# Attention feeding two MoE layers on one Trainium2 core: reciprocals one head later, transfers re-ordered, a third buffer pair, constants on GpSimd, an early weight split

## The chip, the cores and the metric

The kernel runs as one program on one core of a Trainium2 chip. The metric is the device time of one execution in microseconds: the median of three runs of the kernel before is 2205.02 us (2204.62 to 2205.92). Engines are named as in the profile: PE is TensorE, PEld its weight loads, DVE is VectorE, ACT is ScalarE, POOL is GpSimd, SP issues the transfers.

## The reference

Three parts, one behind the other, in float32 (moe_w_in and moe_w_out arrive as float64):

```python
# attention: B=4, H=8, S=576, D=64; a query sees the keys of its own and of earlier blocks of 64
scores = where(block_i >= block_j, q @ k.T / sqrt(D), -1e9)
attn = exp(scores - max(scores));  attn = attn / (sum(attn) + 1e-9);  out = attn @ v
# first MoE: x (2304, 512), w_in (512, 2048), w_out (2048, 512)
h = x @ w_in;  x = (h * cos(h)) @ w_out
# second MoE: 8 experts of width 1024, gates P from a softmax and 8 rounds of row and column normalisation
out = sum_e P[:, e] * (max(x @ w1[e], 0) @ w2[e])
```

## The kernel before, in words

**Order.** The program is written in the order in which each engine executes it; every engine works off its own instructions in that order and waits by semaphores for what an instruction reads, or for the last reader of what it overwrites. All transfers of the attention are issued from SP, also in that order, so a transfer that has to wait holds up those behind it.

**Precision.** Products are made from a rounded high part and a low part (the rest), in three passes (`mm3`, lines 469 to 472), so a matrix needs a high part (ACT as a rule) and a subtraction for the low part (POOL or DVE; `split`, line 61).

**Attention** (lines 147 to 463) takes the 32 heads one by one, in pairs: the even head h=0 and the odd head h=1 of a pair fill the upper and lower 64 rows of x. For head i:

- `load` brings q and k of a head, three heads ahead, into one of two buffers `st`; `load_v` brings v one head ahead.
- `high_parts` (ACT, and POOL for k into KA), `low_parts` (DVE) and `move_k_hi`, `move_k_lo`, `move_q_hi` (transfers between partitions) prepare the operands QA, KA, QB, KB of head i+2; there are two of each, slot i % 2. KA and QA also hold constants (mask, selectors) that `constants` writes once for each slot.
- `peak` is a cheap product into PSUM tile px, `find` on DVE reduces it to maxima, `turn` transposes them on PE, and `maxima` on DVE puts them as extra rows into QA, so that the score product itself subtracts them. That is done for head i+1 while head i runs. px is one buffer: the second group of `peak` waits for the first group's `find`.
- `weights` makes the scores in four parts, each with a first product (KB, QB; line 294) and a second (KA, QA; line 295, which needs the maxima) and an exponential on ACT. `pv` multiplies by v; one more column of ones gives the sums of the exponentials.
- `evac` copies the result to a RAW buffer (two pairs of buffers, by the pair's number), `sums` writes the row of sums to DRAM. Once a pair is complete, `fetch` reads both rows of sums back spread over 72 partitions (tile SC), `invert` takes the reciprocal on DVE, `give` writes them to DRAM, `spread` reads them back to all rows (tile RB, two transfers), `scale` multiplies RAW by RB into XF (DVE, one instruction for each half), and `x_hi` (ACT) and `x_lo` (POOL) split XF into the x of the MoE part.

The main loop is lines 408 to 455. In it, fetch and invert of a pair e stand in head e+2, invert behind the operands of the next head and right ahead of `maxima`; give and spread stand in head e+3, the two scales in heads e+4 and e+5, x_hi and x_lo in head e+5.

**Conversion.** The first MoE's weights arrive as 64-bit floats. `Conv` turns them into float32 in 32 half chunks, each by a load, two ACT, three DVE and one POOL instruction; its generator gives four steps for a half chunk, and `some(n)` takes n steps. Two steps fall into each head and five into each of the first units of the MoE part. Two scratch buffers alternate.

**Opening** (lines 385 to 407): loads, constants of slot 0 on DVE, the first head's operands and maxima, constants of slot 1 and further constants on DVE, then `turn(0)` and `maxima(0)`.

**First MoE** (lines 646 to 780): 48 units, each a block of 768 tokens by 128 columns of w_in: `hidden` twice (12 matmuls each into a buffer h, of which there are two), `reduce_h`, `sine` and `times` for h cos(h), then `o_part` adds the unit before to the output. `wsplit` splits weight chunks; the first stands at line 716, after the attention, followed by `gate_prep`, whose DVE instructions need the gate's transfer (line 487). What remains of the last pairs is done by the `leftover` steps at the ends of units 0 to 5 (lines 461 to 463).

**Second MoE**: from about 680 us on, not touched by the change.

Of the kernel before, what the change touches and what calls it, by code (L numbers as in the profile page):

```python
# [42 lines left out]
def attention_moe_kernel(ctx: ExitStack, tc: tile.TileContext, qk, v, w_a, gate, w_b, out):  # L43
# [10 lines left out]
    eps = top.tile([128, 2], F32, name="eps")  # L54
    nc.vector.memset(eps, 0.0)


# [9 lines left out]

    raw = [None] * F1


    NHALF = 2 * F1

    class Conv:
# [20 lines left out]
        def magnitude(self, k):  # L94

            self.sc[k] = self.scratch(1, k, [128, DM])
            nc.scalar.activation(self.sc[k].bitcast(F32), self.high(k).bitcast(F32), AF.Abs)
# [29 lines left out]
        def run(self):  # L127

            for k in range(NHALF):
                self.magnitude(k)  # L130
                self.rounding(k)
                if 0 < k < NHALF - 1:
                    self.load(k + 1)
                yield
                self.clamp(k)
                yield
                self.shift(k)
                yield
                self.bits(k)
                self.add(k)  # L140
                yield
# [5 lines left out]
    def attention():  # L147
        with tc.tile_pool(name="at1", bufs=1) as p1, tc.tile_pool(name="at2", bufs=2) as p2, \
# [21 lines left out]
            tla = post.tile([128, 6 * TB], F32, tag="tl", name="tla", bufs=1)  # L170
            RAW = [[tla[:, 2 * DM:2 * DM + S], p1.tile([128, S], F32, name="raw")],
                   [tla[:, 2 * DM + S:2 * DM + 2 * S], tt[0][:, 0:S]]]
            RB, XF = tt[1][:, 0:S], tt[2][:, 0:S]
            conv = Conv(post.tile([128, 4 * DM], I32, tag="th", name="cw", bufs=1), tla[:, 0:2 * DM].bitcast(I32))
            conv_gen = conv.run()
# [23 lines left out]

            def constants(slots):  # L200
                nc.vector.memset(diag, 0.0)
                step = [ident[64:72, a:a + 4].unsqueeze(2).to_broadcast([8, 4, 64]) for a in (64, 68)]
                blocks = lambda t, h: t[64:72, 64:576].rearrange("p (t h n) -> p t h n", h=2, n=64)[:, :, h, :]
                shifted = diag[64:72, 64:576].rearrange("p (t h n) -> p t h n", h=2, n=64)
                nc.vector.tensor_copy(out=shifted[:, :, 0, :], in_=step[1])
                nc.vector.tensor_copy(out=shifted[:, :, 1, :], in_=step[0])
                for j in slots:
                    nc.vector.tensor_copy(out=QA[j][:, 0:64], in_=diag[:, 0:64])
                    nc.vector.tensor_copy(out=QA[j][64:96, 64:640], in_=diag[64:96, 64:640])
                    nc.vector.tensor_scalar(out=KA[j][64:128, :], in0=diag[64:128, 0:S], scalar1=0.0, scalar2=None,  # L210
                                            op0=ALU.mult)
                    for h in range(2):
                        nc.vector.tensor_scalar(out=blocks(KA[j], h), in0=step[1 - h], scalar1=MASK, scalar2=None,
                                                op0=ALU.mult)
                    nc.vector.tensor_scalar(out=KA[j][96:101, :], in0=diag[96:101, 0:S], scalar1=-1.0, scalar2=None,
                                            op0=ALU.add)
                    nc.vector.memset(NM[j], 0.0)

            def more_constants():
                nc.vector.tensor_copy(out=diag[96:101, :].rearrange("p (t n) -> p t n", n=128),  # L220
                                      in_=ident[96:101, 96:101].unsqueeze(2).to_broadcast([5, 5, 128]))
                nc.vector.memset(V[0][:, :, D:D + 1], 1.0)
                nc.vector.memset(V[1][:, :, 0:D], 0.0)
                nc.vector.memset(V[1][:, :, 0:1], 1.0)

# [117 lines left out]
            def evac(i):  # L343
                m = D + 1 if i % 2 == 0 else 2 * D
                t = RAW[i // 2 % 2][i % 2]
                nc.scalar.activation(t[0:m], ps_o.pop(i)[0:m, 448:1024], AF.Identity, bias=eps[0:m, i % 2:i % 2 + 1])

            def sums(i):
                t, s = RAW[i // 2 % 2][i % 2], SUM[i % 2]
# [23 lines left out]
            def scale(e, h):  # L373
                r = slice(64 * h, 64 * h + 64)
                nc.vector.tensor_tensor(out=XF[r, :], in0=RAW[e // 2 % 2][h][r, :], in1=RB[r, :], op=ALU.mult)

# [13 lines left out]
            load_v(1)  # L390
            nc.scalar.activation(eps[:, 0:1], eps[:, 0:1], AF.Exp)
            constants([0])
            first_head()
            find(*peak(0, 0))
            find(*peak(0, 1))
            constants([1])
            high_parts(1)
            low_parts(1)
            more_constants()
            nc.vector.memset(eps, 0.0)  # L400
            nc.vector.memset(eps[D:D + 1, 0:1], EPS)
            nc.vector.memset(eps[0:1, 1:2], EPS)
            turn(0)
            maxima(0)
            move_k_hi(1)
            move_k_lo(1)
            load(2)
            for i in range(NH):
                nxt, even, odd = i + 1 < NH, i % 2 == 0, i % 2 == 1
# [46 lines left out]
            evac(NH - 1)  # L456
            e = NH - 2
            sums(NH - 1)
            scale(e - 2, 0)
            scale(e - 2, 1)  # L460
            return conv_gen, {0: lambda: (x_hi(e - 2), fetch(e)), 1: lambda: (invert(e), give(e), x_lo(e - 2)),
                              2: lambda: spread(e), 4: lambda: (scale(e, 0), scale(e, 1), x_hi(e)),
                              5: lambda: x_lo(e)}

    with tc.manual_schedule():
# [180 lines left out]
        def moe1():  # L646
            nonlocal th, tl, C0
            with tc.tile_pool(name="m1", bufs=2) as p, tc.tile_pool(name="pacc", bufs=1, space=PSUM) as pacc:
# [66 lines left out]

                wsplit(0, 0, nc.vector)
                gate_prep()
# [18 lines left out]
                for n in range(NU + 1):  # L736
# [253 lines left out]
```

## Time and profile before

| | |
|---|---|
| median of three runs | 2205.02 us |
| profiled execution | 2205.72 us |
| its span, first to last instruction | 2203.9 us |
| mean granted clock of TensorE | 0.993 |
| PE / PEld / DVE / ACT / POOL busy | 98 / 86 / 68 / 43 / 39 % |
| attention (first to last score product) | 16.6 to 250.5 us |
| first product of the MoE part | 258.4 us |

Busy shares are of the whole span. In the rows, a number in square brackets is the time for which the engine was idle just before, with what ended it. A granted clock of 1.00 is TensorE at 2.4 GHz, 0.50 would be a stretch wholly at 1.2 GHz, and values between are mixtures.

### The profile page before, as it was taken

How to read it: one execution, taken by the hardware profiler on the slowest of the kernel's cores; microseconds unless marked ns; L12 is line 12 of the kernel's file. 1: busy time of each engine (PE TensorE's matmuls, PEld its weight loads, DVE VectorE, ACT ScalarE, POOL GpSimd, SP SyncE). 2: the span in 40 equal slices, each digit the busy share in tenths (PEclk: the TensorE clock that was granted, in tenths of full speed). 3: DMA queues.
4: the chain of work that ended last, by engine and by line, in shares of the span. 5: the costliest groups of instructions: out<-in, count | busy, mean ns of one | idle time of the engine just before them, and what ended most of it. 6: DMA issues, size and time to landing. Idle time of an engine off the chain costs nothing.

```text
span 2203.9 us, 29623 instructions
## 1 busy us (share of the span) xinstructions
PE 2150.4 (98%) x10869; PEld 1889.4 (86%) x10869; DVE 1497.8 (68%) x2464; ACT 957.5 (43%) x1792; POOL 867.5 (39%) x766
## 2 busy tenths in 40 slices
PE   7888899999999999999999999999999999999999
PEld 5666689999898888888888888888888888888887
DVE  6777688666566876666767666666777666666665
ACT  5666555434444343433434434343434343433342
POOL 1222355333332343434563434343554343434341
PEclk9999999999999999999999999999999999999999
DMA  5676421000001121212122212121212221212120
GB/s 144 173 181 175 112 73 58 1 1 10 29 20 39 58 77 58 77 58 77 58 77 87 77 58 77 58 77 58 77 58 88 76 77 58 77 58 77 58 77 29
DMA packets 76641, 157.42 MB, mean 71 GB/s; under 512 B 33392, under 2 KB 33392, under 8 KB 76496
## 3 DMA queue, kind: packets, MB, share of 16 engines
q1 hardware_dynamic: 76496, 155.52, 23.1%
q8 instruction: 86, 1.41, 0.3%
q14 instruction: 59, 0.48, 0.1%
HBM read 136.91 MB, written 4.87 MB: 64 GB/s over the span
## 4 chain that ended last, share of the span: by engine, by line
PE 77%; DVE 7%; issue 7%; DMA 3%; ACT 3%; POOL 3%; SPq 1%; ACTq 0%; POOLq 0%; DVEq 0%
PE acc L470 12%; PE acc L472 12%; PE acc L471 12%; PE hx L472 6%; PE hx L470 6%; PE hx L471 6%; PE hy L472 3%; PE hy L470 3%; PE hy L471 3%; PE acc L701 3%; POOL jl L66 3%; DMA kb<-qb 1%; PE hz L470 1%; PE hz L472 1%; PE hz L471 1%
## 5 line engine op out<-in xcount | busy, mean ns | idle before, releaser
L580 POOL TENSOR_TENSOR wv<-stg,wv 128x512 fp32r<-128x512 f32 x190 | 333.7, 1778 | 858.5 <-ACT wv L579 858.5
L470 PE MATMUL acc<-wv,hh 128*128 128x512 f32 x1152 | 456.5, 396 | 0.0
L472 PE MATMUL acc<-wv,hl 128*128 128x512 f32 x1152 | 455.5, 395 | 0.0
L471 PE MATMUL acc<-wv,hh 128*128 128x512 f32 x1152 | 454.5, 395 | 0.0
L874 DVE SCALAR_TENSOR_TENSOR oa<-acc,P,oa 128x512 f32<-128x512 f32 x540 | 379.0, 740 | 4.9 <-PE acc L472 4.3
L845 ACT ACTIVATE hh<-c 128x384 fp32r<-128x384 f32 x288 | 151.4, 526 | 408.7 <-DVE c L930 167.8
L846 DVE SCALAR_TENSOR_TENSOR hl<-c,hh 128x384 fp32r<-128x384 f32 x288 | 164.0, 570 | 176.5 <-ACT hh L845 176.5
L472 PEld LDWEIGHTS acc<-wv,hl 128*128 128x128 f32 x1152 | 216.0, 187 | 53.7
L471 PEld LDWEIGHTS acc<-wv,hh 128*128 128x128 f32 x1152 | 215.9, 187 | 43.8
L470 PEld LDWEIGHTS acc<-wv,hh 128*128 128x128 f32 x1152 | 216.1, 188 | 43.0
L66 POOL TENSOR_TENSOR jl<-raw,jh 128x512 fp32r<-128x512 f32 x95 | 135.4, 1443 | 240.5 <-ACT jh L63 225.9
L923 DVE TENSOR_TENSOR c<-hz,c 128x384 f32<-128x384 f32 x96 | 53.5, 557 | 193.2 <-PE hz L472 193.2
L571 DVE TENSOR_TENSOR wal<-s,wah 128x1024 fp32r<-128x1024 f32 x96 | 171.4, 1785 | 0.0
L913 ACT ACTIVATE c<-hx 128x384 f32<-128x384 f32 x95 | 46.9, 493 | 275.5 <-PE hx L472 275.5
L470 PE MATMUL h<-xh,jh 128*128 128x384 f32 x384 | 130.5, 340 | 5.7 <-ACT jh L63 3.0
L472 PE MATMUL h<-xh,jl 128*128 128x384 f32 x384 | 129.9, 338 | 1.9 <-POOL jl L66 1.9
L673 ACT ACTIVATE r<-r,half_pi 128x384 f32<-128x384 f32 x96 | 59.2, 617 | 165.5 <-DVE r L668 164.7
L472 PE MATMUL hy<-xh,wal 128*128 128x384 f32 x384 | 128.8, 335 | 0.9 <-DVE wal L571 0.9
L471 PE MATMUL h<-xl,jh 128*128 128x384 f32 x384 | 129.2, 337 | 0.0
L470 PE MATMUL hx<-th,wah 128*128 128x384 f32 x384 | 128.6, 335 | 0.5 <-ACT c L913 0.5
L470 PE MATMUL hy<-xh,wah 128*128 128x384 f32 x384 | 128.7, 335 | 0.4 <-DVE c L930 0.2
L472 PE MATMUL hx<-th,wal 128*128 128x384 f32 x384 | 128.5, 335 | 0.0
(213 smaller groups left out, 4822.1 us busy)
## 6 DMA issues: line engine op xcount, KB each, us to landing
stg<-in_w_b_dram SPq DMA_DIRECT2D x192, 512.0 KB
cw<-in_w_a_dram SPq DMA_DIRECT2D x32, 512.0 KB
st<-in_qk_dram SPq DMA_DIRECT2D x64, 144.0 KB
v<-in_v_dram SPq DMA_DIRECT2D x31, 160.0 KB
tt<-inv SPq DMA_DIRECT2D x32, 144.0 KB
out_dram<-oa SPq DMA_DIRECT2D x18, 256.0 KB
kb<-hi SPq DMA_DIRECT2D x31, 144.0 KB
kb<-qb SPq DMA_DIRECT2D x31, 144.0 KB
```

The source lines that it names most:

```text
L66: eng_lo.tensor_tensor(out=lo, in0=src, in1=hi.bitcast(F32), op=ALU.subtract)
L470: nc.tensor.matmul(ps, lh, rh, start=first, stop=False, skip_group_check=go_on)
L471: nc.tensor.matmul(ps, lh, rl, start=False, stop=False, skip_group_check=go_on)
L472: nc.tensor.matmul(ps, ll, rh, start=False, stop=last, skip_group_check=go_on)
L571: eng.tensor_tensor(out=self.al, in0=self.s, in1=self.ah.bitcast(F32), op=ALU.subtract)
L580: eng.tensor_tensor(out=t[:, DM:2 * DM], in0=src, in1=t[:, 0:DM].bitcast(F32), op=ALU.subtract)
L673: nc.scalar.activation(r, r, AF.Sin, bias=half_pi)
L701: nc.tensor.matmul(acc[half, b][:, at:at + w_], w[:, s], h[:, t0:t0 + w_], start=f == 0 and i == 0 and at == 0, stop=f == F1 - 1 and i == ...
L845: nc.scalar.activation(hh, src, AF.Relu)
L846: nc.vector.scalar_tensor_tensor(out=hl, in0=src, scalar=0.0, in1=hh.bitcast(F32), op0=ALU.max, op1=ALU.subtract)
L874: nc.vector.scalar_tensor_tensor(out=o, in0=acc, scalar=p, in1=o, op0=ALU.mult, op1=ALU.add)
L923: nc.vector.tensor_tensor(out=c[0], in0=z, in1=c[0], op=ALU.add)
```

## The change

- `invert` moves from the even head e+2 (ahead of `maxima`) to the odd head e+3, behind the first `find` on DVE, with `give` right after it. `fetch` stays in head e+2, now ahead of `move_k_lo`; `spread` goes to the end of head e+3's transfers.
- `scale` of the first half moves to the end of head e+4, of the second half to the first part of head e+5; `x_hi` and `x_lo` to head e+6. RAW has three pairs of buffers, and room for them comes from one conversion scratch buffer instead of two and from a slot of the `post` pool.
- `load_v` and `load` stand at the head's start, ahead of `sums` and `move_q_hi`.
- The conversion's steps are cut differently (rounding with the clamp, bits with the shift, add alone), and the loop takes them at other places: one step fewer in head 0.
- In the opening the constants of slot 1, and the ones of v, are written by POOL; the selector tile is made once, the low part of head 1 comes after `maxima(0)`.
- The first weight chunk is split during head 31 into a part of x (xh and xl) that is written only later; the second chunk's split stands ahead of unit 0's products. The leftover steps of the last three pairs are spread over units 1 to 9.

```diff
@@ Conv.run
                 self.magnitude(k)
-                self.rounding(k)
                 if 0 < k < NHALF - 1:
                     self.load(k + 1)
                 yield
+                self.rounding(k)
                 self.clamp(k)
                 yield
                 self.shift(k)
+                self.bits(k)
                 yield
-                self.bits(k)
                 self.add(k)
                 yield
...
@@ opening
+            nc.scalar.activation(SC[:, 0, 0:1], half_pi[0:72, :], AF.Exp)
+            selectors()
+            constants(0, nc.vector)
+            constants(1, nc.gpsimd)
             first_head()
-            find(*peak(0, 0))
+            px = peak(0, 0)
+            tiles()
+            find(*px)
             find(*peak(0, 1))
-            constants([1])
             high_parts(1)
-            low_parts(1)
-            more_constants()
+            ones_of_v()
...
             turn(0)
             maxima(0)
+            low_parts(1)
             move_k_hi(1)
             move_k_lo(1)
             load(2)
@@ main loop, head i
                 if i:
                     evac(i - 1)
-                if odd and i >= 3:
-                    give(i - 3)
+                    if nxt:
+                        load_v(i + 1)
+                if i + 3 < NH:
+                    load(i + 3)
                 if i:
                     sums(i - 1)
+                if even and i:
+                    some(1)
                 if nxt:
                     move_q_hi(i + 1)
-                if i and nxt:
-                    load_v(i + 1)
-                if nxt:
                     find(*peak(i + 1, 0))
                 for part in range(4):
                     weights(i, part)
-                if i >= 4:
-                    scale(i - 4 - i % 2, i % 2)
+                if odd and i >= 3:
+                    invert(i - 3)
+                    give(i - 3)
+                if odd and i >= 5:
+                    scale(i - 5, 1)
                 if nxt:
                     find(*peak(i + 1, 1))
+                if nxt2:
+                    high_parts(i + 2)
+                    move_k_hi(i + 2)
+                if even and i >= 2:
+                    fetch(i - 2)
+                if nxt2:
+                    low_parts(i + 2)
+                    move_k_lo(i + 2)
                 if odd and i >= 3:
                     spread(i - 3)
-                if i + 3 < NH:
-                    load(i + 3)
-                if even and i >= 2:
-                    fetch(i - 2)
-                if i + 2 < NH:
-                    high_parts(i + 2)
-                    move_k_hi(i + 2)
-                    low_parts(i + 2)
-                    move_k_lo(i + 2)
-                if even:
-                    some(1)
-                elif i >= 5:
-                    x_hi(i - 5)
-                    x_lo(i - 5)
-                if even and i >= 2:
-                    invert(i - 2)
-                if odd:
-                    some(1)
+                if even and i >= 6:
+                    x_hi(i - 6)
+                    x_lo(i - 6)
+                if i == NH - 1:
+                    split(*spare, raw[0][:, 0:DM], nc.scalar, nc.gpsimd)
+                some(1)
                 pv(i, 0)
                 pv(i, 1)
...
-                some(1)
+                if even and i >= 4:
+                    scale(i - 4, 0)
+                if odd:
+                    some(1)
@@ after the loop
+            return conv_gen, {1: lambda: (x_hi(e - 4), x_lo(e - 4)), 2: lambda: scale(e - 2, 0),
+                              3: lambda: (scale(e - 2, 1), x_hi(e - 2), fetch(e)),
+                              4: lambda: (x_lo(e - 2), invert(e), give(e)), 5: lambda: spread(e),
+                              7: lambda: scale(e, 0), 8: lambda: (scale(e, 1), x_hi(e)), 9: lambda: x_lo(e)}
@@ first MoE
-                wsplit(0, 0, nc.vector)
+                wj[0, 0] = spare
                 gate_prep()
...
+                        if n == 0:
+                            wsplit(1, 0)
                         pa = hidden(*w, t0)
                         ra = reduce_h(pa)
                         pb = hidden(*w, t0 + TB)
                         sine(ra)
-                        wsplit(n + 1, 0)
+                        if n:
+                            wsplit(n + 1, 0)
```

The new `selectors`, `constants(j, eng)`, `tiles` and `ones_of_v` hold the instructions of the former `constants` and `more_constants`, with the engine as an argument; `constants` is seven instructions for a slot, of 64, 576, 576, 256, 256, 576 and 101 columns.

## Rows read from the trace of the kernel before

**Rows 1.** Page, part 1: busy us (share of the span) and instructions of each engine.
```profile
PE 2150.4 (98%) x10869; PEld 1889.4 (86%) x10869; DVE 1497.8 (68%) x2464; ACT 957.5 (43%) x1792; POOL 867.5 (39%) x766
```

**Rows 2.** Stretches: length, busy of PE, PEld, DVE, ACT, POOL; clock, DMA share, GB/s.
```profile
108.85:116.11 7.26, 6.18 (x33) 3.99 (x31) 4.57 (x10) 5.05 (x9) 1.92 (x2) 1.00 0.63 138
...
101.02:108.85 7.83, 7.83 (x31) 6.18 (x32) 6.23 (x12) 4.58 (x8) 2.11 (x3) 0.78 0.72 215
245.00:250.45 5.45, 5.45 (x29) 3.68 (x28) 4.31 (x10) 3.17 (x7) 1.10 (x1) 1.00 0.55 147
25.45:250.45 225.00, 199.57 (x928) 141.57 (x927) 158.76 (x297) 140.91 (x251) 60.09 (x57) 0.94 0.67 171
...
262.23:366.77 104.54, 100.25 (x560) 91.31 (x559) 91.81 (x145) 57.46 (x104) 57.05 (x41) 1.00 0.24 74
366.77:467.00 100.23, 100.23 (x576) 92.14 (x576) 62.36 (x115) 44.11 (x82) 37.20 (x26) 1.00 0.00 1
```

**Rows 3.** Waits from 20 to 280: who waited for whom; us, times, longest.
```profile
DVE sc L358 <- DMA sc<-sums: 42.8, 15, 4.9
...
PE sp L295 <- DVE qa L286: 25.4, 14, 3.7
```

**Rows 4.** Timeline of heads 12 and 13: start, us, engine, line, operation, tiles.
```profile
108.81 1.29 DVE L277 TENSOR_REDUCE nm<-px 128x1 f32<-128x448 f32 x2
...
110.53 0.54 PE L261 MATMUL px<-ka,qa 68*128 68x256 f32 x3
...
111.11 0.89 DVE L277 TENSOR_REDUCE nm<-px 128x1 f32<-128x192 f32 x3 [0.35 <-PE px L261]
...
111.85 0.68 ACT L228 ACTIVATE qa<-st 64x576 fp32r<-64x576 f32 x1
...
111.92 0.75 DVE L233 TENSOR_TENSOR qb<-st,hi 128x576 fp32r<-128x576 f32 x1
...
112.59 0.50 SPq L355 DMA_DIRECT2D sc<-sums  x1
...
114.94 0.25 DVE L358 RECIPROCAL sc<-sc 72x16 f32<-72x16 f32 x1 [2.28 <-DMA sc<-sums]
115.22 0.31 SPq L362 DMA_DIRECT2D inv<-sc  x1
115.22 0.83 DVE L286 TENSOR_TENSOR qa<-pt,diag 5x640 fp32r<-5x640 f32 x1
...
116.09 0.43 DVE L108 TENSOR_SCALAR tla<-tla 128x512 f32<-128x512 f32 x1
...
117.86 0.76 DVE L375 TENSOR_TENSOR tt<-raw,tt 64x576 f32<-64x576 f32 x1
...
118.73 1.11 SPq L367 DMA_DIRECT2D tt<-inv  x2
...
121.56 1.04 DVE L119 SCALAR_TENSOR_TENSOR raw<-cw,tla 128x512 int32<-128x512 int32 x1
```

**Rows 5.** Timeline of the opening.
```profile
6.66 1.40 POOL L252 TENSOR_TENSOR qb<-st,hi 64x576 fp32r<-64x576 f32 x1
...
8.12 0.66 POOL L229 CAST ka<-st 64x576 fp32r<-64x576 f32 x1
...
12.64 1.36 PE L261 MATMUL px<-ka,qa 68*128 68x256 f32 x3 [1.94 <-DVE ka L213]
...
16.58 0.79 PE L295 MATMUL sp<-qa,ka 101*128 101x512 f32 x1 [2.16 <-DVE qa L286]
```

**Rows 6.** Timeline of the step into the MoE part.
```profile
254.85 1.28 POOL L125 TENSOR_TENSOR raw<-raw,cw 128x512 int32<-128x512 int32 x1
...
254.93 1.81 DVE L375 TENSOR_TENSOR tt<-tla,tt 64x576 f32<-64x576 f32 x1 [2.55 <-POOL xl L382]
...
256.44 0.40 SPq L487 DMA_DIRECT2D g<-in_gate_dram  x1
...
258.36 0.69 PE L470 MATMUL h<-xh,jh 128*128 128x384 f32 x1 [3.01 <-ACT jh L63]
```

More of the change, by code (lines that the diff above doesn't have):

```diff
@@ L55, in attention_moe_kernel @@
     nc.vector.memset(eps, 0.0)
+    nc.vector.memset(eps[D:D + 1, 0:1], EPS)
+    nc.vector.memset(eps[0:1, 1:2], EPS)
     xh = top.tile([128, NC, N], F32R, name="xh")
@@ L68, in attention_moe_kernel @@
     raw = [None] * F1
+    spare = [x[:, NC - 1, (B - 1) * S:(B - 1) * S + DM] for x in (xh, xl)]
     NHALF = 2 * F1
@@ L94, in magnitude @@
         def magnitude(self, k):
-            self.sc[k] = self.scratch(1, k, [128, DM])
+            self.sc[k] = self.own[1]
             nc.scalar.activation(self.sc[k].bitcast(F32), self.high(k).bitcast(F32), AF.Abs)
@@ L170, in attention @@
             tla = post.tile([128, 6 * TB], F32, tag="tl", name="tla", bufs=1)
-            RAW = [[tla[:, 2 * DM:2 * DM + S], p1.tile([128, S], F32, name="raw")],
-                   [tla[:, 2 * DM + S:2 * DM + 2 * S], tt[0][:, 0:S]]]
+            odd_raw = (post.tile([128, S], F32, tag="lt", name="rawl", bufs=1), p1.tile([128, S], F32, name="raw"),
+                       tt[0][:, 0:S])
+            RAW = [[tla[:, DM + j * S:DM + (j + 1) * S], odd_raw[j]] for j in range(3)]
             RB, XF = tt[1][:, 0:S], tt[2][:, 0:S]
-            conv = Conv(post.tile([128, 4 * DM], I32, tag="th", name="cw", bufs=1), tla[:, 0:2 * DM].bitcast(I32))
+            conv = Conv(post.tile([128, 4 * DM], I32, tag="th", name="cw", bufs=1), tla[:, 0:DM].bitcast(I32))
             conv_gen = conv.run()
@@ L198, in load_v, with selectors @@
                     nc.sync.dma_start(out=vt[0:64, 4, c], in_=v[b, h, 512:S, :])
-            def constants(slots):
+            def selectors():
                 nc.vector.memset(diag, 0.0)
-                step = [ident[64:72, a:a + 4].unsqueeze(2).to_broadcast([8, 4, 64]) for a in (64, 68)]
-                blocks = lambda t, h: t[64:72, 64:576].rearrange("p (t h n) -> p t h n", h=2, n=64)[:, :, h, :]
                 shifted = diag[64:72, 64:576].rearrange("p (t h n) -> p t h n", h=2, n=64)
[L205 to L217, printed above, removed]
@@ L219, in more_constants, with step, constants @@
-            def more_constants():
+                for h in range(2):
+                    nc.vector.tensor_copy(out=shifted[:, :, h, :], in_=step(1 - h))
+            def step(h):
+                return ident[64:72, 64 + 4 * h:68 + 4 * h].unsqueeze(2).to_broadcast([8, 4, 64])
+            def constants(j, eng):
+                eng.tensor_copy(out=QA[j][:, 0:64], in_=diag[:, 0:64])
+                eng.tensor_copy(out=QA[j][64:96, 64:640], in_=diag[64:96, 64:640])
+                eng.tensor_scalar(out=KA[j][64:128, :], in0=diag[64:128, 0:S], scalar1=0.0, scalar2=None,
+                                  op0=ALU.mult)
+                for h in range(2):
+                    out = KA[j][64:72, 64:576].rearrange("p (t h n) -> p t h n", h=2, n=64)[:, :, h, :]
+                    eng.tensor_scalar(out=out, in0=step(1 - h), scalar1=MASK, scalar2=None, op0=ALU.mult)
+                eng.tensor_scalar(out=KA[j][96:101, :], in0=diag[96:101, 0:S], scalar1=-1.0, scalar2=None,
+                                  op0=ALU.add)
+                eng.memset(NM[j], 0.0)
@@ L220, in more_constants, with tiles, ones_of_v @@
+            def tiles():
                 nc.vector.tensor_copy(out=diag[96:101, :].rearrange("p (t n) -> p t n", n=128),
                                       in_=ident[96:101, 96:101].unsqueeze(2).to_broadcast([5, 5, 128]))
-                nc.vector.memset(V[0][:, :, D:D + 1], 1.0)
-                nc.vector.memset(V[1][:, :, 0:D], 0.0)
-                nc.vector.memset(V[1][:, :, 0:1], 1.0)
+            def ones_of_v():
+                nc.gpsimd.memset(V[0][:, :, D:D + 1], 1.0)
+                nc.gpsimd.memset(V[1][:, :, 0:D], 0.0)
+                nc.gpsimd.memset(V[1][:, :, 0:1], 1.0)
@@ L344, in evac @@
                 m = D + 1 if i % 2 == 0 else 2 * D
-                t = RAW[i // 2 % 2][i % 2]
+                t = RAW[i // 2 % 3][i % 2]
                 nc.scalar.activation(t[0:m], ps_o.pop(i)[0:m, 448:1024], AF.Identity, bias=eps[0:m, i % 2:i % 2 + 1])
             def sums(i):
-                t, s = RAW[i // 2 % 2][i % 2], SUM[i % 2]
+                t, s = RAW[i // 2 % 3][i % 2], SUM[i % 2]
                 if i % 2 == 0:
@@ L374, in scale @@
                 r = slice(64 * h, 64 * h + 64)
-                nc.vector.tensor_tensor(out=XF[r, :], in0=RAW[e // 2 % 2][h][r, :], in1=RB[r, :], op=ALU.mult)
+                nc.vector.tensor_tensor(out=XF[r, :], in0=RAW[e // 2 % 3][h][r, :], in1=RB[r, :], op=ALU.mult)
             def x_hi(e):
@@ L408, in attention @@
             for i in range(NH):
-                nxt, even, odd = i + 1 < NH, i % 2 == 0, i % 2 == 1
+                nxt, nxt2, even, odd = i + 1 < NH, i + 2 < NH, i % 2 == 0, i % 2 == 1
                 if i:
                     evac(i - 1)
-                if odd and i >= 3:
-                    give(i - 3)
+                    if nxt:
+                        load_v(i + 1)
+                if i + 3 < NH:
+                    load(i + 3)
                 if i:
                     sums(i - 1)
+                if even and i:
+                    some(1)
                 if nxt:
                     move_q_hi(i + 1)
-                if i and nxt:
-                    load_v(i + 1)
-                if nxt:
                     find(*peak(i + 1, 0))
@@ L454, in attention @@
                     pv(i, c)
-                some(1)
+                if even and i >= 4:
+                    scale(i - 4, 0)
+                if odd:
+                    some(1)
             evac(NH - 1)
+            sums(NH - 1)
             e = NH - 2
[L458 to L463, printed above, removed]
+            return conv_gen, {1: lambda: (x_hi(e - 4), x_lo(e - 4)), 2: lambda: scale(e - 2, 0),
+                              3: lambda: (scale(e - 2, 1), x_hi(e - 2), fetch(e)),
+                              4: lambda: (x_lo(e - 2), invert(e), give(e)), 5: lambda: spread(e),
+                              7: lambda: scale(e, 0), 8: lambda: (scale(e, 1), x_hi(e)), 9: lambda: x_lo(e)}
     with tc.manual_schedule():
```

5 lines of the change are left out of this document (removed).

## The prediction

> **What bounds the kernel now.** I read the page first: TensorE is busy 98% of the span [rows 1], so the time moves only where TensorE idles or runs at its lower clock. The stretches show where that is [rows 2]. From head 1's second score product (25.45) to head 31's (250.45) lie 225.00 us; TensorE is busy 199.57 of them at a mean granted clock of 0.94. In the first MoE part the twelve units from 366.77 on take 100.23 us without a gap, the twelve before them 104.54. What a head needs is in the same view: head 12 has 6.18 us of matmuls at clock 1.00, yet lasts 7.26; head 30, which prepares no further maxima, 5.45; head 11, behind a stall, takes 7.83 at clock 0.78. The waits name the stall [rows 3]: fifteen times VectorE stands before the reciprocal (42.8 us) for the transfer that brings the sums back, and the score product waits for the maxima behind it on VectorE (25.4 us). One instance is in the timeline of heads 12 and 13 [rows 4]: the fetch is issued at 112.59, the reciprocal can start only at 114.94, the maxima at 115.22.
>
> **The attention loop.** (1) The reciprocal moves from the even head into the following odd one, behind the first maxima reduction. The fetch stays where it was, 3.74 us into the even head (112.59 against that head's start 108.85). Landing 2.35 us after issue [rows 4], it arrives 6.1 us in; the new place comes up at 6.18 + 1.25 = 7.4 us, so 1.3 us are to spare. The loop's idle, 225.00 - 199.57 = 25.43 us [rows 2], goes; with the stalls gone the clock should stay at its upper level, which takes the busy time to 29 x 6.18 + 5.45 = 184.67. Floor: 184.67 instead of 225.00, -40.33.
>
> (2) What is late next? VectorE's busy time is 158.76 us in the fifteen pairs of heads [rows 2], 10.58 per pair against TensorE's 2 x 6.18 = 12.36, so VectorE isn't the bound by its sum. Its order is tight, however. In an even head the scale of a pair's first half now stands behind the maxima and must wait for GpSimd's low part of x, which follows ScalarE's chain: q's high part ends at 112.53, 3.68 into the head [rows 4]; the high part of x takes as long again (0.68), the low part on GpSimd 1.40 (the price of [rows 5]'s subtraction): 5.8 us in. From there VectorE's path runs to the release of the px buffer for the next even head: scale 0.76, two reductions 1.29, reciprocal 0.25, scale 0.76, three reductions 0.89, k and q low parts 0.75, clamp 0.43, maxima 0.83, shift 0.43, bits 0.69 to 1.04, two reductions 1.29 [rows 4], together 8.4 to 8.7. TensorE wants that buffer 1.68 us into the next even head (in head 12 the second px group starts at 110.53), at 12.36 + 1.68 = 14.0; VectorE gives it at 14.2 to 14.5. So a pair takes 0.2 to 0.5 us over 12.36, and I take 0.4. If the GpSimd cast of k (0.66, [rows 5]) falls on the scale, one of the two waits: up to 0.75 in all. At nothing the pair is 12.36. The loop: -40.33 + 15 x 0.4 = -34.3, bounds -40.3 and -29.
>
> (3) The order on SP costs nothing by itself. The same transfers are issued, about 9.6 us per pair out of 12.7. v's load and the loads three heads on move to the head's start; both buffers they overwrite are free by then. Behind them stand the sums, then q's high part, which the next head needs. Its issue comes about 1 us later in the head than before, near 2; with the 2.35 of a landing and some queueing it is there by 4.6 us of 6. Spreading the reciprocals now ends an odd head: give is issued some 2 us in, and in [rows 4] spread follows give by 3.51 (115.22 to 118.73), so SP is free at 2.2 + 3.5 + 1.1 = 6.8, 0.6 into the next head, which the 1.4 us of slack cover. The third buffer pair only lets the scale come later. The conversion's single scratch is rewritten two steps after its last read; one step of 64 moves into the MoE part.
>
> **The opening.** The score product of head 0 starts at 16.58 after 2.16 us of waiting for maxima, and the px group before it at 12.64 after 1.94 of waiting for the constants of slot 1 [rows 5], which VectorE wrote between the two. On GpSimd those seven instructions have 2405 columns: at the cast's 0.66 per 576 2.8 us, at the subtraction's 1.40 per 576 5.8 us. They start near 2 us and end at 4.8 to 7.8; the two subtractions of head 0 (1.40 each, formerly done by 8.06) end at 8.0 to 10.6, ScalarE's two high parts of head 1 (0.68 each) at 9.4 to 12.0. TensorE is free for px at 12.64 - 1.94 = 10.7, so px starts at 10.7 to 12.0. The score product could formerly start at 16.58 - 2.16 = 14.42, 1.78 after px; now that is 12.5 to 13.8, the maxima being ready by about 11.5. Gain 2.8 to 4.1; I take 3.3. Bounds: 5 if the upper clock also comes earlier, 0 if the two engines hinder each other for the whole 2.8 us. That they can is in [rows 6]: the scale at 254.93 took 1.81 instead of 0.76, ending 0.61 after a GpSimd instruction that began just before it. The Trainium skill, page "Advanced Engine Details and Errata", section "VectorE Performance Modes", says the second VectorE port is shared with GpSimd, so that two-port VectorE instructions and GpSimd ones block each other. The row agrees; by that rule alone the opening gains 0.5 and the time is 2168.
>
> **The step into the MoE part.** TensorE idles 3.01 us before 258.36 for ScalarE's split of the first weight chunk [rows 6]; with the chunk split during head 31 it starts at once, at 255.35. But VectorE's first work there is the gate's preparation, which needs a transfer issued at 256.44, after the last evacuation. Taking the fetch's 2.35 for it, it lands at 258.8, and four small instructions (0.65) end at 259.45. The reduction of unit 0, which starts the stretch at 262.23 [rows 2], starts there: -2.8. TensorE has run out of unit 0's products by then (half of a unit's 8.35, at 259.5) and idles about 2 us until unit 1's buffer is free. Bounds: -4.8 without that wait, -1.5 if the stall lowers the clock again.
>
> **Units 2 to 13.** They lose 104.54 - 100.23 = 4.3 now. Two more scales (0.76 each) and one more GpSimd low part join VectorE's 91.81 of 104.54, but one per unit where two stood together. I take 0; bounds -2 and +3.
>
> **The sum.** -34.3 - 3.3 - 2.8 + 0 = -40.4. The profiled execution took 2205.72 us, 1.8 more than its span and 0.7 more than the median of the three runs: 2165.3 there, 2164.6 against the median. I predict 2165. All lower bounds: -40.3 - 5 - 4.8 - 2 = -52, 2153; the upper, the opening's set at 1: -29 - 1 - 1.5 + 3 = -28.5, 2176.
>
> **Rivals.** (a) TensorE alone binds: pairs of 12.36, and the rest as forecast: 2159; with the lower bounds elsewhere 2153. For it: VectorE's 10.58 per pair. Against: the path above leaves nothing over. Chance 0.08.
> (b) A transfer keeps half of the stall: pairs of about 14.0, with clock losses. Faster heads ask the DMA engines for 171 x 15.0 / 12.7 = 202 GB/s; the sums' issue now stands behind two loads and v, and the fetch waits for its landing. If the fetch comes 1.5 us later and takes 3.5 (as some of the 15 waits, up to 4.9, suggest), the reciprocal waits 1.4. Loop -15, rest -6: 2184. Chance 0.13.
> (c) It doesn't do what it says: the sums come so late that VectorE still waits as long, one head later. This needs a round trip over 3.7 us after issue each time; [rows 4] show 2.35. Then only opening, step and some clock are gained: 2195. Chance 0.05.
> (d) Slower: SP's spread waits for give's landing, and v, the loads, the sums and q's high part of the next head queue behind it. From give's issue (2.2) the chain is L, then 1.1 spread, 2.4 of issues, 2.35 landing, and it must end at 12.1: it costs TensorE from L = 4.0 on, and eats the whole 40 us (2.7 a pair) from L = 6.7. Against: 3.51 in [rows 4] is an upper value of L. At L = 7 the time is 2210. Chance 0.04.
>
> **Chances.** The forecast, 2154 to 2176, has 0.70; with half of (b) and nearly all of (a) the range 2153 to 2182 holds 8 in 10. A measurement of this kernel tells about 0.2% from no change. Faster by more 0.95 (forecast, a, b, c), within it 0.01, slower 0.04 (d).
>
> **What would show it.** Right: reciprocals with no idle before them; heads of 6.2 to 6.5 us at clock 1.00; some waiting of px for VectorE in even heads; the first score product near 13; no gap before unit 0 but one of about 2 us before unit 1. Wrong: q's transfer or SP's spread among the waits of TensorE, GpSimd's low part of x as the longest wait of VectorE, a clock under 1 in the loop, or px of head 1 after 12.6.

## The result, and the profile after

The changed kernel takes 2177.16 us (median of four runs, 2175.55 to 2178.88) against 2205.18 (2204.62 to 2205.92) for the kernel before, run beside it: a ratio of 0.9873, 95% interval 0.9856 to 0.9890. The forecast was 2165, range 2153 to 2182: right in sign and inside the range, but 12 us too fast, and the measured time lies above the 2154 to 2176 of the forecast itself. Each row below is of one profiled execution, which can lie some us from its kernel's median. The one of the change took 2176.37, 29.35 less than the one before; the forecast said 40.4.

The page's line of the engines, against [rows 1]:

```profile
PE 2138.5 (98%) x10869; PEld 1879.6 (86%) x10869; DVE 1490.3 (69%) x2449; ACT 957.5 (44%) x1792; POOL 873.8 (40%) x777
```

The stretches that answer to [rows 2], with the same columns: head 0, the loop from head 1's second score product to head 31's, heads 13 and 14, the step into the MoE part, units 2 to 13, and the twelve units behind them:

```profile
15.14:22.67 7.53, 7.53 (x32) 5.56 (x31) 4.09 (x9) 4.67 (x8) 0.66 (x1) 1.00 0.59 147
...
22.67:223.77 201.10, 190.56 (x928) 132.24 (x927) 156.31 (x295) 141.22 (x251) 59.10 (x57) 0.99 0.76 191
104.30:111.68 7.38, 6.49 (x33) 4.62 (x31) 7.16 (x15) 4.53 (x8) 1.74 (x2) 1.00 0.87 215
111.68:118.29 6.61, 6.27 (x33) 4.09 (x31) 3.37 (x7) 5.08 (x9) 2.45 (x3) 1.00 0.67 162
223.77:233.24 9.47, 9.26 (x48) 7.54 (x46) 4.14 (x10) 5.97 (x10) 3.82 (x3) 1.00 0.18 57
233.24:338.10 104.86, 98.82 (x549) 90.87 (x550) 90.22 (x146) 57.07 (x104) 55.59 (x40) 0.98 0.24 75
338.10:437.70 99.60, 99.60 (x573) 91.55 (x572) 62.67 (x115) 43.90 (x82) 37.02 (x26) 1.00 0.02 6
```

The difference of the two executions splits along these ends. Up to head 1's second product: 25.45 to 22.67, -2.8. The loop: 225.00 to 201.10, -23.9. From there to unit 0's reduction: 250.45 to 262.23 was 11.78, now 9.47, -2.3. Units 2 to 13: 104.54 to 104.86, +0.3. The twelve units behind them -0.6. Nearly all that is missing is missing in the loop, where the forecast had 190.7 and 201.10 was measured: 13.4 us for a pair of heads in the mean, not 12.7. TensorE idles 10.54 us there (before 25.43), at a clock of 0.99 (0.94).

Who waits there now, from 20 to 225 (engine and line, for whom, us, times, longest; SPq is SP's own queue):

```profile
DVE nm L285 <- PE px L269: 26.5, 20, 4.0
...
DVE tt L383 <- POOL xl L390: 9.6, 11, 1.0
...
PE sp L302 <- DMA qb<-qa: 6.6, 11, 1.3
...
PE sp L302 <- DMA kb<-hi: 2.1, 3, 1.0
...
SPq L375 <- DMA inv<-sc: 16.8, 13, 2.5
```

The reciprocal's wait of [rows 3] for the sums is gone from the list. In its place the first score product waits for the transfer of q's high part (qb<-qa), and on SP the spread (L375) waits 1.3 us each time for give's landing. Of the signs that the prediction had named as showing it wrong, q's transfer among TensorE's waits has come; spread stands among SP's waits, not TensorE's. The clock is a little under 1, and px of head 1 starts at 13.56 (shown further below), after the 12.6 named. The fourth has not come: GpSimd's low part of x is not VectorE's longest wait (9.6 us, px 26.5). The timeline of heads 13 and 14 has both, beside a reciprocal (L366) that waits for nothing:

```profile
105.54 0.24 DVE L366 RECIPROCAL sc<-sc 72x16 f32<-72x16 f32 x1
...
106.93 0.48 SPq L250 DMA_DIRECT2D qb<-qa  x1
107.50 0.51 SPq L370 DMA_DIRECT2D inv<-sc  x1
...
108.81 0.46 SPq L247 DMA_DIRECT2D kb<-qb  x1
...
111.34 0.50 PE L302 MATMUL sp<-qb,kb 128*128 128x512 f32 x1 [0.89 <-DMA qb<-qa]
...
111.38 1.10 SPq L375 DMA_DIRECT2D tt<-inv  x2
...
114.91 0.48 SPq L250 DMA_DIRECT2D qb<-qa  x1
...
117.95 0.50 PE L302 MATMUL sp<-qb,kb 128*128 128x512 f32 x1 [0.34 <-DMA qb<-qa]
```

SP goes in order. All its lines here are transfers being issued. Give (L370) is issued at 107.50, 3.2 us into head 13; k's low part is away by 109.27; then SP stands until 111.38, because spread may not read what give has not yet written. Everything of head 14 is issued behind it: v at 112.57, q's high part at 114.91, 3.2 us into the head, and the product at 117.95 waits 0.34 for it. In head 13 q was issued 2.6 us in, at a DMA share of 0.87, and took 4.4 us to the product at 111.34, which had waited 0.89.

Over the whole loop most of the loss is like head 13's. Of the 6.6 us of waits for q, 5.8 (8 of 11) belong to a q that was issued in an odd head, behind the load of a 512 KB weight chunk that ends the even head; these took 3.9 to 4.9 us from the issue to the product. The three others, issued in the even heads that follow SP's stand, took 3.0 to 3.2 and cost 0.8 us in all.

### The profile page after: what moved, and what is told of

It reads as the page before. It is cut to its first block, busy times and chain, and to the rows that moved or that the text cites. A ratio compares the mean times of both kernels' runs of the same rounds, so it can differ in the third digit from the quotient of the medians.

```text
span 2174.6 us, 29648 instructions
## 1 busy us (share of the span) xinstructions
PE 2138.5 (98%) x10869; PEld 1879.6 (86%) x10869; DVE 1490.3 (69%) x2449; ACT 957.5 (44%) x1792; POOL 873.8 (40%) x777
## 4 chain that ended last, share of the span: by engine, by line
PE 77%; DVE 7%; issue 6%; POOL 3%; DMA 3%; ACT 3%; SPq 0%; ACTq 0%; POOLq 0%; DVEq 0%
PE acc L480 12%; PE acc L482 12%; PE acc L481 12%; PE hx L482 6%; PE hx L480 6%; PE hx L481 6%; PE hy L482 3%; PE hy L480 3%; PE hy L481 3%; PE acc L711 3%; POOL jl L68 3%; DMA qb<-qa 2%; PE hz L480 2%; PE hz L481 1%; PE hz L482 1%
## 5 line engine op out<-in xcount | busy, mean ns | idle before, releaser
L481 PE MATMUL hy<-xl,wah 128*128 128x384 f32 x384 | 128.3, 334 | 0.0
```

The costliest lines, as they stand in the source:

```text
L481: nc.tensor.matmul(ps, lh, rl, start=False, stop=False, skip_group_check=go_on)
```

## The experiments

Theory 1: q's transfer is issued too late within its head, behind v, the loads and the sums. Theory 2: SP's stand before the spread makes it late. Theory 3: the traffic makes each landing long, the 512 KB chunk loads above all. All ratios are against the kernel before, run beside. The runs are compared by these ratios, as they are from several chips; 0.001 is 2.2 us.

**q's transfer ahead of v.**

```diff
+                if nxt:
+                    move_q_hi(i + 1)
+                if i and nxt:
+                    load_v(i + 1)
...
-                    move_q_hi(i + 1)
                     find(*peak(i + 1, 0))
```

> The changed kernel with the transfer of q's high part issued first in a head, ahead of v, the two loads and the sums. Theory 1 (order: q stands behind 450 KB of loads on SP and in the DMA engines): the score products' waits for q and k high parts (24 us in the changed kernel's loop, weight loads and products together) vanish, the loop of 201.1 us falls to about 190, the time from 2177 to about 2166. Theory 2 (SP stands still for the landing of the reciprocals ahead of spread): q is still late in the heads after spread, so at most half of it, 2171. Theory 3 (the DMA engines are simply full because of the 512 KB weight chunk): the queue is as long whatever stands first in it, 2175 to 2177.

Measured: 2191.58, ratio 0.9946 (0.9929 to 0.9963), some 15 us slower than the change (0.9873). Its waits from 22 to 222:

```profile
DVE sc L366 <- DMA sc<-sums: 18.7, 13, 2.7
...
SPq L250 <- DMA kb<-qb: 23.5, 25, 1.9
```

Theory 1's cure is worse than the ailment; TensorE's own waits for q fall only from 6.6 to 3.6 us. q's high part goes into the rows of QB that the transfer of k's low part (kb<-qb) is still reading, so an earlier q stands on SP until that has landed, in nearly every head, and holds back the sums; the reciprocals wait again. In the change v, the two loads and the sums are issued in that time, and q stands for k's low part only once (0.3 us). So Theory 1 isn't refuted: q is late, but put ahead of v it only stands there.

**The spread an even head later, behind q.**

```diff
                     move_q_hi(i + 1)
+                if even and i >= 4:
+                    spread(i - 4)
...
-                if odd and i >= 3:
-                    spread(i - 3)
```

> The changed kernel with spread taken out of the end of the odd head and issued in the next even head, behind q's high part (the last pair's but one in unit 1). Theory 2: SP no longer waits about 1.3 us per pair for the reciprocals' landing, the transfers of even heads come 1.5 to 2.5 us earlier, q's waits of even heads vanish: 2171. Theory 1: q of the odd heads still stands behind v, loads and the chunk, which is where the longer waits are; gain below 4 us: 2174. Theory 3: no gain, 2177. A loss is possible if the spread now lands after the scale wants it (VectorE waits for RB): 2180.

Measured: 2169.23 (2166.16 to 2170.66), ratio 0.9846 (0.9832 to 0.9861). The loop:

```profile
22.50:213.25 190.75, 187.50 (x928) 131.59 (x927) 157.28 (x295) 140.94 (x251) 58.85 (x57) 1.00 0.79 203
```

and what is left of TensorE's waits for q:

```profile
PE sp L302 <- DMA qb<-qa: 0.7, 3, 0.3
```

Theory 2 holds: with nothing changed but the spread's place, the loop takes 190.75 us, where 190.7 had been forecast, and of TensorE's waits for q 0.7 us are left (6.6 in the change), at more traffic than in the change (203 GB/s, 191 there). SP's delay reached the odd heads too: there q is issued 2.3 us into the head in the mean in the change, 1.8 in this run. Two things temper the number. The profiled execution took 2166.16, 3 us less than the median; by the ratios the gain over the change is some 6 us, and the two intervals overlap a little. And the same loop, in the profiled execution of the run "on top of the later spread" below, took 194.74. So what the spread's place gives back of the loop's 201.10 is 6 to 10 us.

**Both at once**: q and then the spread ahead of v.

```diff
+                if nxt:
+                    move_q_hi(i + 1)
+                if even and i >= 4:
+                    spread(i - 4)
+                if i and nxt:
+                    load_v(i + 1)
...
-                    move_q_hi(i + 1)
...
-                if odd and i >= 3:
-                    spread(i - 3)
```

> Both: q's high part first in a head, then in even heads the spread, then v, loads and sums. Theories 1 and 2 together: no wait for q at all and no idle SP; loop about 188 to 190, pairs of 12.5 to 12.6, time 2164 to 2166; if theory 1 alone holds, the same as the kernel with q first (2166). Theory 3: 2175 or more.

Measured: 2207.71, ratio 1.0020 (1.0011 to 1.0029). SP stands 42.2 us for k's low part before q (26 times), VectorE 21.2 for the sums and 13.2 for the spread (tt<-inv, 8 times), which it did not wait for with q alone. The whole gain is lost. q's place accounts for some 16 us of it, as in the first run. The other 16 are the spread's, which gave 6 in the run before: there it stood behind v, the loads, the sums and q; here it stands between a q that waits and all of these. How the two act together no run here separates.

**Fourteen of the 32 half chunks not loaded.** The loads of the attention loop are left out, so the first MoE part works on other weights than the given ones.

```diff
+            if 2 <= k < 16:
+                return
             src = w_a[k // 2]...
```

> The changed kernel without 14 of the 32 loads of weight chunks (those of half chunks 2 to 15, 512 KB each, which fall into the attention loop); the conversion runs on what its buffers hold, so the first MoE's weights are wrong. Theory 3: the waits for q vanish, loop 190, time about 2166. Theory 1: the odd heads' q no longer has the chunk ahead of it, but v, loads and sums still are: half of the waits, 2171. Theory 2: even heads' q stays late, 2173.

Measured: 2165.65, ratio 0.9832 (0.9818 to 0.9847); the loop takes 189.72, and TensorE no longer waits for q at all. Theory 3 holds too. Taking away the chunks removes the whole loss, and taking away SP's stand most or all of it: with short landings (the spread follows give by 2.7 us in the mean, 3.4 in the change) SP's stand is short (2.2 us in all, 16.8 in the change), and without the stand q is early enough for long landings. This run takes away the 0.5 us that each load costs SP as well; that it is the traffic and not this is likely from the landings, but the two weren't tried apart.

**The reciprocal back in the even head**, the rest as changed.

```diff
                 if odd and i >= 3:
-                    invert(i - 3)
                     give(i - 3)
...
+                if even and i >= 2:
+                    invert(i - 2)
                 pv(i, 0)
```

> The changed kernel with one part undone: the reciprocal stands again in the even head, behind the operands of the next head and right ahead of the maxima; give stays in the odd head. If the reciprocal's place is what took the stall away (the forecast's main step), VectorE waits again 2 to 4 us for the sums in each of 15 even heads, the loop is back at 220 to 235 us, and the time at 2195 to 2210. Rival: the re-ordered transfers and the third buffer pair are the gain; then the time stays under 2185.

Measured: 2186.81, ratio 0.9922 (0.9908 to 0.9937). Its loop, and its waits from 22 to 238:

```profile
22.11:237.71 215.60, 196.41 (x928) 134.27 (x928) 159.94 (x296) 141.32 (x252) 58.96 (x57) 0.98 0.73 179
```

```profile
DVE sc L366 <- DMA sc<-sums: 33.5, 15, 3.4
...
PE sp L303 <- DVE qa L294: 14.1, 14, 1.7
```

The stall of [rows 3] is back, at about half its price to TensorE (14.1 us in place of 25.4). The profiled execution took 2190.59, 4 us more than the median: by its row the moved reciprocal is worth 14.5 us of the loop as long as the other edits stand, by the ratios 11. That is less than I had expected, and the time is just over the rival's 2185: the other edits of the loop give at least the 9.4 that are left, by themselves. Which of them, no run tells.

**The move alone, in the kernel before.**

```diff
-                if odd and i >= 3:
-                    give(i - 3)
...
                     find(*peak(i + 1, 0))
+                if odd and i >= 3:
+                    invert(i - 3)
+                    give(i - 3)
...
-                if even and i >= 2:
-                    invert(i - 2)
```

> The kernel before with the reciprocal and give alone moved behind the first maxima reduction of the odd head; spread stays where it was, in the middle of the odd head. If the reciprocal's place alone counts: loop about 195 to 200 us, time about 2178. If SP's wait for the landing of give counts (shown by the run with spread a head later), SP stands still for about 3 us in the middle of each odd head, ahead of the next load and the next head's k parts, and a part of the gain is lost: 2185 to 2195.

Measured: 2221.83, ratio 1.0076 (1.0059 to 1.0093): slower than before. The loop takes 240.55, and these are its waits from 22 to 222:

```profile
ACT hi L227 <- DMA kb<-hi: 34.9, 14, 4.4
...
DVE sc L358 <- DMA sc<-sums: 14.0, 11, 1.7
...
SPq L242 <- DMA kb<-qb: 35.9, 24, 2.7
SPq L367 <- DMA inv<-sc: 20.1, 11, 2.1
```

The reciprocal still waits, but the maxima no longer stand behind it (TensorE's wait for them falls from 25.4 us to 0.3), and yet the loop is 15.6 us longer. This is the mechanism of rival (d): give comes later, the spread stands on SP for it, and k's and q's moves queue behind. So the move of the reciprocal pays only together with the other edits of the loop: they turned +15.6 into a gain of 11 to 14.5. The order of the transfers on SP, which the prediction had at nothing, is the likely one by the waits; the later scale, the third buffer pair and the conversion's steps weren't tried one by one.

**On top of the later spread: the gate's load in the opening, slot 1's constants on VectorE between the first two maxima groups.**

```diff
-            constants(1, nc.gpsimd)
             first_head()
-            px = peak(0, 0)
-            tiles()
-            find(*px)
+            find(*peak(0, 0))
+            constants(1, nc.vector)
             find(*peak(0, 1))
+            tiles()
...
+            nc.sync.dma_start(out=g0, in_=gate...)   # ahead of the head loop
```

> Spread in the next even head as before, and two more edits, read in their own stretches. (1) The gate's transfer is issued in the opening: VectorE's gate preparation no longer waits for it, unit 0's reduction starts when its products are done, and the gap of 2.75 us before unit 1 falls under 0.6. (2) The constants of slot 1 are written by VectorE between the first two maxima reductions: constants of slot 0 take 0.45 again instead of 0.9 each, px(0,0) starts near 5.3 instead of 6.9, the first second score product near 13.5 instead of 15.14 if the shared port and the wait for GpSimd's last constant were the cause; if GpSimd's subtractions bound the opening, not before 15. Time about 2164 against 2169.

Measured: 2165.44 (2163.74 to 2166.44), ratio 0.9823 (0.9808 to 0.9838). In its timeline a constant of slot 0, head 0's first maxima group and second score product, and unit 1's first product:

```profile
2.30 0.45 DVE L216 CAST qa<-diag 32x576 fp32r<-32x576 bf16 x1
...
5.35 1.38 PE L270 MATMUL px<-ka,qa 68*128 68x256 f32 x3 [5.35 <-DVE qa L257]
...
13.68 0.73 PE L304 MATMUL sp<-qa,ka 101*128 101x512 f32 x1
...
225.88 0.41 PE L482 MATMUL h<-xh,jh 128*128 128x384 f32 x1 [0.55 <-DVE g L687]
```

The opening gains a further 1.5 us, and the gap before unit 1, 2.75 in the change, shrinks to 0.55: the score product of head 0 is now 2.9 us ahead of [rows 5], so the 3.3 forecast for the opening was nearly to be had, though not with the constants on GpSimd. The total tells less (the intervals of this run and of the later spread alone overlap), because the loop of this execution is longer, at the same instructions:

```profile
21.34:216.08 194.74, 188.28 (x928) 131.47 (x927) 157.61 (x295) 140.73 (x251) 58.04 (x57) 1.00 0.77 197
```

TensorE waits 3.2 us for q in it (6 times, all issued in odd heads), where 0.7 were left before.

**x's split in the odd head too**, on top of that.

```diff
-                if even and i >= 6:
-                    x_hi(i - 6)
-                    x_lo(i - 6)
+                if odd and i >= 5:
+                    x_hi(i - 5)
+                    x_lo(i - 5)
```

> The kernel just described with the high and low part of x in the odd head (e+5) instead of the next even one. The forecast held that VectorE's path over GpSimd's low part of x costs 0.2 to 0.5 us per pair over the floor of 12.36. If so, the loop of 190.75 us falls by 3 to 6 us and the time to about 2160. If the path isn't the bound, nothing changes.

Measured: 2164.09 (2163.13 to 2166.35), ratio 0.9819 (0.9805 to 0.9834): not told apart from the one before. VectorE's wait for GpSimd's low part of x (9.1 us in the run before) is gone, and the loop takes 190.81 us, no less than the 190.75 that was had with this wait: it was not the bound. This is the shortest time of the study, some 12 us under the change by the ratios.

**Two more places on SP**, on top of that: q between v and the loads; and the chunk's load behind the spread in the even head.

```diff
                         load_v(i + 1)
+                if nxt:
+                    move_q_hi(i + 1)
                 if i + 3 < NH:
...
-                    move_q_hi(i + 1)
```

```diff
                     spread(i - 4)
+                    conv.load(i // 2 + 1)
```

> On the last kernel (spread later, gate early, opening's constants on VectorE, x in the odd head): q's high part issued behind v and ahead of the two loads and the sums. What is left of TensorE's waits in the loop is q (some 2 us in all). If the 288 KB of loads ahead of it hold it up, the waits go: loop 190.8 to 187 or 188, time about 2161. If, as with q first, SP then stands for the landing of k's low part and the sums come later, the loop grows: 2166 to 2175.

> On the same kernel: the 512 KB load of the weight chunk moved from the end of the even head to its middle, behind q's high part and spread, so that it isn't the last thing ahead of the odd head's v, loads and q. If the chunk's packets hold up the odd heads' q (as the run without chunk loads suggests), TensorE's waits for q go and the loop falls by 1 to 3 us: 2161 to 2163. If it then holds up the fetch of the sums and k's parts instead, the reciprocal waits: 2166 or more.

Measured: 2188.68, ratio 0.9918 (0.9904 to 0.9932), and 2187.06, ratio 0.9924 (0.9912 to 0.9937). Each gives away some 22 or 23 us by the ratios. In the first:

```profile
DVE tt L384 <- DMA tt<-inv: 15.0, 12, 3.1
...
SPq L251 <- DMA kb<-qb: 36.3, 27, 2.7
```

and in the second:

```profile
DVE sc L367 <- DMA sc<-sums: 16.4, 11, 3.0
...
SPq L251 <- DMA kb<-qb: 21.3, 13, 2.9
```

Both make q stand on SP for k's low part: the first by issuing q sooner, the second by putting 512 KB in front of k's transfer (its 13 stands are in the odd heads, behind a chunk loaded in the even one).

## Why the prediction was right, and where it was short

**The stall that goes.** Right: the reciprocals wait for nothing, and the clock of the loop is 0.99. Putting the reciprocal back brings the waits back. But the sum gave the whole -40.3 to this one move; made alone it costs 15.6.

**What VectorE's order adds (0.4 a pair).** The sum is met where SP is out of the way (190.75 against 190.7), but by luck: two errors cancel, and the same loop took 194.74 in another execution. TensorE's busy time is 187.50 at clock 1.00, not the 184.67 extrapolated from two heads, and its idle time 3.25, not 6. TensorE's waits for VectorE before px are 2.4 us of this, so VectorE adds about 0.2 a pair. The waits named are there and small: px for VectorE 1.5 us in the change, VectorE for GpSimd's low part of x 9.6, and taking that away (x's split in the odd head) changed nothing.

**The order on SP.** This is the step that failed: "The order on SP costs nothing by itself." It was mis-sized at 0; the loop is 10.4 us over the forecast, and putting the spread later takes back 6 to 10 of them. Three numbers of it were off. Give goes out 3.2 us into the head, not 2.2. Spread follows give by 3.88 in head 13, beyond the 3.51 of [rows 4], which rival (d) took for an upper value; it wasn't one: in the kernel before the fifteen times are 1.92 to 4.29, the longest from 219.13 to 223.42. And in heads 13 and 14 q is issued 2.6 and 3.2 us in and takes 4.4 and 3.0 us to its product, where the 2.35 of the small fetch in [rows 4] had been used, with "some queueing". Rival (d) had the mechanism and set its threshold at a give-to-spread time of 4.0; the pairs lost 0.7 us each at 2.97 to 4.25, above 4.0 only once. With 3.2 for its 2.2 and 3.0 for its 2.35 its own sum gives a threshold of 2.4, as an estimate. The argument took each transfer by itself; the two delays add on one queue. That the time still fell inside the range is luck: 2177 is beyond the forecast's upper bound, and the range reached further only for half of rival (b), late sums, which did not come.

**The opening (-3.3).** Half right, and the -2.8 near it partly luck. The first second score product came at 15.14 against 16.58, -1.4, under the 2.8 to 4.1 worked out. Head 0 then took 7.53 us where it had taken 8.87, another -1.3, which the sum did not hold (only its bound of 5 did). The same product of head 0, in the kernel before and in the change:

```profile
20.43 1.91 PE L328 MATMUL o<-ep,v 128*65 128x512 f32 x2
```

```profile
18.72 1.02 PE L336 MATMUL o<-ep,v 128*65 128x512 f32 x2
```

In both, head 0's score products of 256 columns take 0.41 us and head 1's 0.28; the product shown is still a long one in the kernel before and already a short one in the change. Before, TensorE had stood idle for 2.16 us ahead of the product at 16.58; now it works without a break from 13.27 on. This looks like the upper clock coming earlier, which the bound of 5 spoke of, but the column of the granted clock says 1.00 for both stretches, so that is not shown. The reason for the shortfall of the 1.4 is in the timeline:

```profile
2.30 0.87 DVE L215 CAST qa<-diag 32x576 fp32r<-32x576 bf16 x1
...
2.93 1.76 POOL L216 TENSOR_SCALAR ka<-diag 64x576 fp32r<-64x576 bf16 x1
...
4.77 2.36 POOL L220 TENSOR_SCALAR ka<-ident 8x256 fp32r<-8x256 f32 x2
...
6.93 1.38 PE L269 MATMUL px<-ka,qa 68*128 68x256 f32 x3 [6.93 <-DVE qa L256]
7.20 1.65 POOL L221 TENSOR_SCALAR ka<-diag 5x576 fp32r<-5x576 bf16 x1
...
8.88 0.82 DVE L226 CAST diag<-ident 5x640 bf16<-5x640 f32 x1 [2.00 <-POOL ka L221]
...
13.56 1.35 PE L269 MATMUL px<-ka,qa 68*128 68x256 f32 x3
...
15.14 0.63 PE L303 MATMUL sp<-qa,ka 101*128 101x512 f32 x1
```

The last of these constants on GpSimd ends at 8.85, past the forecast's 4.8 to 7.8, and the same constants of slot 0 on VectorE are slower beside them: the cast takes 0.87, where with VectorE alone it takes 0.45. So head 0's first group starts at 6.93, not 5.35. Then VectorE's next cast, which overwrites the diag tile that GpSimd's last constant reads, waits 2.00 for it, a wait not in the working; head 0's maxima stand behind it. The rule of the Trainium skill that the prediction weighed (page "Advanced Engine Details and Errata", section "VectorE Performance Modes": GpSimd and two-port VectorE instructions block each other) is borne out in sign by these rows; the 0.5 us of gain worked out from it was too pessimistic against 1.4. Which of VectorE's instructions here are two-port ones, no row says.

**The step (-2.8).** Measured -2.3; what holds it is what was forecast, the gate's transfer and then unit 1.

```profile
228.59 0.44 PE L480 MATMUL h<-xh 128*128 128x384 f32 x1
...
229.74 0.40 SPq L497 DMA_DIRECT2D g<-in_gate_dram  x1
...
231.28 1.31 POOL L128 TENSOR_TENSOR raw<-raw,cw 128x512 int32<-128x512 int32 x1
...
231.67 0.96 DVE L67 CAST ghl<-g 128x32 fp32r<-128x32 f32 x1 [5.04 <-DMA g<-in_gate_dram]
...
233.24 0.56 DVE L676 TENSOR_SCALAR ki<-h 128x384 int32<-128x384 f32 x1
...
235.78 0.41 PE L480 MATMUL h<-xh,jh 128*128 128x384 f32 x1 [2.75 <-DVE g L687]
```

No gap before unit 0's products, as forecast; the gap before unit 1 is 2.75, forecast about 2. The 0.5 that lacks is VectorE's: the transfer is there after 1.93 us, not 2.35, but the four small instructions behind it take 1.57 us, from 231.67 to 233.24, not 0.65. The first of them, a cast of 0.17 in the kernel before, takes 0.96 and ends at 232.63, just behind the GpSimd instruction that began before it and ended at 232.59. The prediction had weighed such a hindrance in the opening only.

**Units 2 to 13.** Forecast 0, measured +0.3.

## What to carry to other kernels

A queue that issues in order is an engine: a transfer whose source or target isn't free yet holds up every later one, so list each transfer's wait, and put independent transfers in front of those that must wait. When a wait is moved later, follow the transfers that hang on it; here the same move cost 15.6 us by itself and gave 11 to 14.5 with the other edits in place. A landing time read at one place of a waiting loop can be too short for the faster loop (2.35 us was taken, 3.0 to 4.9 came): look at all of them and take the longest, not the one beside the stall.

## What the runs showed of the hardware that was not expected

GpSimd's constants cost far more than by the column: 1.65 to 1.76 us for 576 columns of a scalar product from bf16, where its cast of 576 columns takes 0.66, from bf16 as from fp32; 5 partitions cost as much as 64. VectorE stood idle while the one of 1.65 ran, so it was not slowed by VectorE. The VectorE instructions beside such constants double (0.45 to 0.87), and a cast of 0.17 beside a GpSimd instruction took 0.96. And the 144 KB move of q within the SBUF took, from its issue to a product that waited for it, 3.0 to 4.9 us: 4.4 in head 13, at a DMA share of 0.87, and 3.0 in head 14, at 0.67.
